# A scan whose later groups keep one PSUM bank instead of reseeding it, with a new instruction order and a one-engine last token

## The chip, the cores and the metric

The kernel runs on one core of a Trainium2 chip (trn2). The metric is the device time of one execution in microseconds (us), the median over several executions. A core has five engines that run their own instruction streams side by side: TensorE (PE, matmuls, with weight loads shown apart as PEld), VectorE (DVE), ScalarE (ACT), GpSimd (POOL) and SyncE (SP, which here only starts transfers). Matmul results go to PSUM, which this kernel treats as eight banks of 512 float32 per partition; ACT and DVE copy them from there to SBUF.

## The reference

Two independent computations over the same length of 2048 tokens and width of 448; their outputs stand side by side in one (1, 2048, 896) bf16 tensor. Part A is a diagonal state-space layer with complex state of 448 entries, part B a local attention with 16 heads of 28, a window of 8 and a dilation of 2.

```python
# A
Lam_bar = jnp.exp(dt * Lam)
B_bar = ((Lam_bar - 1.0) / Lam)[:, None] * Bmat
Bu = jnp.einsum("bld,pd->blp", x + 0j, B_bar)
for t in range(L):
    h = Lam_bar[None, :] * h + Bu[:, t, :]
    hs.append(h)
y = 2.0 * jnp.einsum("blp,dp->bld", hseq, Cmat).real + x * Dskip[None, None, :]
# B
qkv = (x @ wqkv)                       # split into q, k, v and heads
idx = pos[:, None] - off[None, :]      # off = 0, 2, ..., 14; idx < 0 is masked
logits = einsum("bhsd,bhswd->bhsw", q, kg) * scale
attn = softmax(logits)
o = einsum("bhsw,bhswd->bhsd", attn, vg);  b = o @ wo
return concatenate([a, b], axis=-1)
```

## The kernel before

**Units and the order.** The program is put together from 614 *units*. `Planner.add` (L129) makes one: the engine that does it (or a tuple of engines that could), costs, a function that issues its instructions, the units that it depends on, and the PSUM banks or buffers that it takes (`acq`) and gives back (`rel`). The costs and priorities are not used when the program is built: `Planner.run` (L163) walks through a list of unit numbers written out by hand, `ORDER` (L46), and issues each unit in that order. So every engine gets its instructions in the sequence in which its units stand there, and each engine works in that sequence: an instruction that waits holds up everything behind it on its engine. An entry of `ORDER` is the unit's number plus 1000 times the position of the chosen engine in its tuple. A second list, `BANKS` (L77), names the PSUM bank (or the first of a pair) for each `Slot` in the order in which they are first taken.

```python
        for x in ORDER:
            u = self.units[x % 1000]
            ...
            u.on = u.eng[x // 1000]
```

**Part B.** Tokens are handled in two halves, b = 0 and 1, with 128 partitions times 8 tokens each. `loads` (L323) brings weights and x in, the x transposed by DMA (L353). `u_wm` (L434) copies the last 64 columns of the q and k weights into a tile of their own, `wm`, for the mixed projection (`first`, L486). `proj` (L439, matmuls in L453) makes q and k; a tile row has 448 = 3 x 128 + 64 entries, so each output has three full matmuls and 64-row remainders that are done in pairs. Evictions go by `evict` and `copy` (L198 to L210; the copies themselves are L202 on ACT, L206 on DVE, scaled ones L204). `dup` (L532, transfers L535 and L537) copies the k and q of column block 3 within the partition range; it is one unit for each half. `qk` (L539) forms the windowed products on DVE (L560) and sums them on PE (L573), `softmax` (L588) follows; its last step, `turn` (L638), is two copies on ACT for each half that bring the attention weights into the order that `pv` needs. `pv` (L710) multiplies by v on DVE (L727), folds the window (L733 and, for the last group, in halves with L744), turns the result by a DMA transpose (L771), multiplies by wo (full matmuls L790, 64-row remainders L797), and evicts and stores through `ev2` (L800) and `out` (L806). Of the last pair of tokens, the first one's copy goes whole to one engine and the second one's is split, columns 0 to 255 by ACT and the last 192 by DVE (L815 to L819).

**Part A.** `loads` and `load_x` bring the parameters and x (xaT_sb); `setup` forms the discretised factors, `u_s` among them (`spair`, `u6c`), `setup_weights` the input matrix `Bcat`. `powers` (L1068) builds, for each group, diagonal matrices of powers of the factors, `pw`, in two units, the first with 5 powers and the second with 10. Each can go to DVE, as one instruction (L1084), or to ACT, as one for each power and half (L1082).

The scan (L1094) runs over seven groups m of 64 complex states, in 16 phases of tokens, of which each matmul handles 512 columns. The phases are four classes: the even pair P (two banks) and the odd classes 1 and 3 (one bank each). For each group:

1. PE forms the input term in the banks (L1135, 64-row remainders L1138), for the pair first;
2. ACT saves the pair as `eP` (L1148); PE adds it, times a power, to the odd banks (`s1`, L1152);
3. ACT saves bank 1 as `e1` (L1156); PE adds it to bank 3 (L1159); ACT saves part of bank 3 (L1163) and PE adds it (L1167 to L1169);
4. five rounds alternate small copies on ACT (`evv`, L1174) and small products on PE (`l2`, L1179), which carry the state over the row; PE spreads the result (`s4`, L1185) and ACT makes the h of class 3 (`ev3`, L1188);
5. *back to class 1*: PE adds the carried state (`s5`, L1191 and L1192) to bank 1, and ACT copies the h of class 1 out (`ev1f`, through L202);
6. *back to the pair*: the same with `s6` and `s7` (L1231) and a copy of 1024 (`evPf`, L202).

Steps 5 and 6 need the values that steps 2 and 3 had left in bank 1 and in the pair. `FIN` (L43) says for each group and for both where they come from. With `"seed"` the bank is given back as soon as it has been saved, and later ACT copies the saved tile into a fresh bank (`back1`, L1199; `back`, L1217), to which PE then adds. With `"hold"` the bank is kept until the final copy and there is no seed:

```python
            hold, holde = mP == "hold", m1 == "hold"
            s1_, sP_ = (sl[1] if holde else sl["b1"]), (sl["P"] if hold else sl["P2"])
```

Before the change all seven groups use `"seed"` for both. The output product (L1319) then multiplies h with C in units of two tokens; for half of the tokens a skip product with the diagonal is done on PE, for the others on DVE. Copies out of PSUM go through `ev`, stores through `out` (L1341), always begun by SyncE. The last token that the program handles is copied in two pieces, 256 columns by ACT and 192 by DVE (near L1371), and both must be done before its store.

Of the kernel before, what the change touches and what calls it, by code (L numbers as in the profile page):

```python
# [42 lines left out]
FIN = (("seed", "seed"),) * 7  # L43
# [32 lines left out]
]  # L76
BANKS = [  # L77
# [235 lines left out]
class PartB:  # L313
# [114 lines left out]
    def prep(self, u_warm):  # L428
# [5 lines left out]
        self.u_wm = P.add("DVE", vec2(896), lambda: nc.vector.tensor_copy(  # L434
            self.wm[:], self.wqk.rearrange("p k (a c) -> p k a c", a=2)[:, :, :, DF:D]),
# [274 lines left out]
    def pv(self, b, prio, deps):  # L710
# [67 lines left out]
        for j0 in range(0, JB, 2):  # L778
# [27 lines left out]
            def out(j0=j0, jb=jb, e0=0, e1=2):  # L806
                nc.sync.dma_start(self.out_b[b][:, j0 + e0:j0 + e1, :], cx.yb_v[:, jb["y"], e0:e1])
                if e1 == 2:
                    cx.yb_ring.put(jb["y"])
# [3 lines left out]
            en = ("ACT", "DVE")  # L813
            if tail:
                v = P.add(en, (act(448), vec(448)), lambda eng, f=ev2: f(eng, e1=1), [us[2], *cx.u_free], pr, acq="yb")  # L815
                o = P.add("SP", 0.45, lambda f=out: f(e1=1), [v], pr, lat=1.1, dma=0.5)
                w = P.add("ACT", act(D - 192), lambda f=ev2: f("ACT", e0=1, c1=D - 192), [us[2], v], pr)
                w2 = P.add("DVE", vec(192), lambda f=ev2: f("DVE", e0=1, c0=D - 192), [us[2], v], pr)
                P.add("SP", 0.45, lambda f=out: f(e0=1), [w, w2, o], pr, rel=(sl, "yb"), lat=1.1, dma=0.5)  # L819
            else:  # L820
                v = P.add(en, (act(896), vec(896)), ev2, us + cx.u_free, pr, rel=sl, acq="yb")
                P.add("SP", 0.45, out, [v], pr, rel="yb", lat=1.1, dma=1.0)


class PartA:
# [483 lines left out]
    def outputs(self, prio):  # L1309
        nc, pool, P, cx = self.nc, self.pool, self.plan, self.cx  # L1310
        for n, j in enumerate(range(0, T, 2)):
# [29 lines left out]
            def out(j=j, jb=jb, j0=0, j1=2):  # L1341
                nc.sync.dma_start(self.out_a[:, j + j0:j + j1, :], cx.ya_v[:, jb["r"], j0:j1])
                if j1 == 2:
                    cx.ya_ring.put(jb["r"])
# [18 lines left out]
            e = lambda f, **k: (lambda eng: f(eng, **k))  # L1363
            if n < 5:
                v = P.add(*en(896), e(ev), us + x + cx.u_free, pr - 2, rel=sl, acq="ya")
                P.add("SP", 0.45, out, [v], pr, rel="ya", lat=1.1, dma=1.0)
            else:
                u = P.add(*en(448), e(ev, j0=0, j1=1), us[:1] + x + cx.u_free, pr - 2, acq="ya")
                o = P.add("SP", 0.45, lambda f=out: f(j0=0, j1=1), [u], pr, lat=1.1, dma=0.5)
                if n < 7:  # L1370
                    v = [P.add(*en(448), e(ev, j0=1, j1=2), [us[1], u], pr - 2, rel=sl)]  # L1371
                else:
                    v = [P.add("ACT", act(256), lambda f=ev: f("ACT", j0=1, j1=2, c1=256), [us[1], u], pr - 2),
                         P.add("DVE", vec(192), lambda f=ev: f("DVE", j0=1, j1=2, c0=256), [us[1], u], pr - 2)]
                P.add("SP", 0.45, lambda f=out: f(j0=1, j1=2), [*v, o], pr, rel=("ya", sl) if n == 7 else "ya", lat=1.1, dma=0.5)


@with_exitstack
# [103 lines left out]
```

## Time and profile before

| | us |
|---|---|
| runs of the kernel | 135.98, 136.2, 134.9 |
| median | 135.98 |
| the profiled execution's own time | 135.03 |
| its span (first to last instruction or packet of the profile) | 133.3 |
| granted TensorE clock over the span, 1 = full | 0.997 |

The profile is that of one execution, the one of 135.03 us; 1.7 us of it lie outside the span. Times in the profile count from the span's start. A group of instructions is named by the engine, the source line (L1135 is line 1135 of the kernel before), the operation, and the tiles written and read with their shapes. "SPq" and "ACTq" are the sequences in which SyncE and ScalarE start transfers; the length shown there is that of starting one, not of the transfer. In a view by time, each row gives the start, the length to the end of the last instruction, the engine, and the count behind an "x"; a bracket at its end says how long the engine stood idle before it and what ended that. A matmul's end is modelled, so the distance from one start to the next is the surer measure of PE's pace.

### The profile page before, as it was taken

What the parts mean: (1) busy time and instruction counts of PE and PEld (TensorE: products, weight loads), DVE (VectorE), ACT (ScalarE), POOL (GpSimd) and SP (SyncE); (2) the same over time, 40 slices, a digit from 0 to 9 for tenths busy, and PEclk for the clock granted to TensorE, in tenths of its full rate; (3) what the DMA queues carried; (4) which work ended last, traced back from release to release, by engine and by line L of the source; (5) the groups of instructions that cost most, each with busy time, mean ns of one, the idle gap of its engine ahead of it and who ended that gap; (6) DMA issues with size and microseconds to landing.
All of it is one profiled execution on the core that took longest, in us unless ns stands there. A gap on an engine that the chain in (4) does not pass through costs nothing.

```text
span 133.3 us, 2479 instructions
## 1 busy us (share of the span) xinstructions
PE 126.8 (95%) x921; PEld 63.4 (48%) x921; DVE 113.4 (85%) x130; ACT 105.4 (79%) x189; POOL 12.1 (9%) x28
## 2 busy tenths in 40 slices
PE   6999989999999999999999899999999999999990
PEld 2477333434546434464454255444566555545430
DVE  5256998999999999999999999999999999992011
ACT  2067968987999957879999999989999649569270
POOL 6940491000000000000000000000000000000000
PEclk9999999999999999999999999999999999999998
DMA  4999949989346758827869988006620685318642
GB/s 91 207 199 186 146 100 232 178 193 201 73 91 104 170 147 290 222 51 152 266 97 143 260 210 244 19 0 138 147 67 0 165 227 199 102 63 219 234 148 93
DMA packets 47759, 20.25 MB, mean 152 GB/s; under 512 B 38774, under 2 KB 46346, under 8 KB 47748
## 3 DMA queue, kind: packets, MB, share of 16 engines
q1 hardware_dynamic: 46676, 19.77, 64.7%
q10 hardware_dynamic: 880, 0.31, 1.2%
q8 instruction: 7, 0.11, 0.4%
q0 software_dynamic: 192, 0.03, 0.1%
q14 instruction: 4, 0.03, 0.1%
HBM read 5.18 MB, written 4.19 MB: 70 GB/s over the span
## 4 chain that ended last, share of the span: by engine, by line
PE 73%; ACT 15%; SPq 5%; DMA 3%; issue 1%; DVE 0%; ACTq 0%
PE banks L1319 16%; PE banks L1135 12%; PE banks L453 10%; PE banks L790 7%; PE banks L673 7%; PE banks L573 6%; SPq L349 4%; PE banks L1179 3%; DMA rb<-in_B_wqkv_dram 3%; ACT qk L202 2%; ACT pbuf L1174 2%; PE banks L1152 2%; ACT h L202 2%; PE banks L797 2%; ACT banks L1217 1%; SPq L360 1%
## 5 line engine op out<-in xcount | busy, mean ns | idle before, releaser
L560 DVE TENSOR_TENSOR prods<-qk 128x4096 bf16<-128x4096 bf16 (+1 forms) x18 | 31.7, 1809 | 0.3 <-ACT qk L202 0.2
L1135 PE MATMUL banks<-xaT_sb,Bcat 128*128 128x512 bf16 (+1 forms) x112 | 26.9, 381 | 0.6 <-ACT h L202 0.6
L202 ACT CAST ra<-banks 128x896 bf16<-128x896 f32 (+2 forms) x24 | 17.9, 773 | 7.8 <-PE banks L797 4.2
L202 ACT CAST qk<-banks 128x512 bf16<-128x512 f32 (+3 forms) x20 | 16.9, 843 | 3.9 <-PE banks L453 1.4
L733 DVE TENSOR_TENSOR prods<-prods 128x7168 bf16<-128x7168 bf16 x4 | 15.6, 3892 | 0.1
L727 DVE TENSOR_TENSOR prods<-ra 128x7168 bf16<-128x7168 bf16 x4 | 15.5, 3886 | 0.0
L727 DVE TENSOR_TENSOR prods<-ra,qk 128x7168 bf16<-128x7168 bf16 x4 | 15.5, 3886 | 0.1
L1319 PE MATMUL banks<-Ccat,h 128*128 128x448 bf16 x64 | 14.7, 353 | 0.0
L453 PE MATMUL banks<-rb 128*128 128x512 bf16 (+1 forms) x64 | 13.3, 379 | 0.6 <-ACT sh L960 0.6
L1135 PEld LDWEIGHTS <-Bcat 128*128 128x128 bf16 (+1 forms) x112 | 9.1, 100 | 9.7 <-issue 3.7
L673 PE MATMUL banks<-wv,rb 128*128 128x448 bf16 (+1 forms) x64 | 13.7, 354 | 0.0
L1319 PE MATMUL banks<-Ccat,qk 128*128 128x448 bf16 x48 | 11.7, 352 | 0.0
L790 PE MATMUL banks<-wo_p,rb 128*128 128x448 bf16 x48 | 10.9, 354 | 0.0
L1174 ACT CAST pbuf<-banks 128x64 bf16<-128x64 f32 (+1 forms) x42 | 9.3, 229 | 0.9 <-PE banks L1179 0.6
L1179 PE MATMUL banks<-pbuf,pw 128*128 128x64 bf16 x77 | 9.7, 235 | 0.2
L204 ACT ACTIVATE qk<-banks 128x512 bf16<-128x512 f32 (+2 forms) x10 | 8.4, 849 | 1.2 <-PE banks L453 1.0
L1179 PEld LDWEIGHTS <-pw 128*128 128x128 bf16 x77 | 6.5, 105 | 5.5 <-issue 1.9
L453 PEld LDWEIGHTS <-rb 128*128 128x128 bf16 (+1 forms) x64 | 5.1, 96 | 7.9 <-issue 2.8
L206 DVE CAST ra<-banks 128x192 bf16<-128x192 f32 x2 | 0.7, 358 | 9.2 <-ACT ra L202 9.2
L1319 PEld LDWEIGHTS <-h 128*128 128x128 bf16 x64 | 5.8, 98 | 5.3 <-issue 0.7
L1084 DVE TENSOR_TENSOR pw<-Dm,spair 128x1280 bf16<-128x1280 bf16 (+1 forms) x13 | 8.0, 664 | 0.0
L1148 ACT CAST eP<-banks 128x1024 bf16<-128x1024 f32 x7 | 7.1, 1014 | 0.9 <-PE banks L1135 0.9
(145 smaller groups left out, 201.8 us busy)
## 6 DMA issues: line engine op xcount, KB each, us to landing
out_dram<-ra SPq DMA_DIRECT2D x12, 224.0 KB, 2.3
xaT_sb<-in_A_x_dram SPq DMA_DIRECT2D x2, 448.0 KB, 4.8
out_dram<-ra SPq DMA_DIRECT2D x8, 112.0 KB, 1.7
ra<-ra SPq DMA_DIRECT2D x2, 392.0 KB, 4.1
qk<-qk SPq DMA_DIRECT2D x2, 392.0 KB, 4.1
wv<-in_B_wqkv_dram SPq DMA_DIRECT2D x2, 336.0 KB, 4.2
ra<-ra SPq DMA_DIRECT2D x1, 588.0 KB
qk<-qk SPq DMA_DIRECT2D x1, 588.0 KB, 5.6
```

Source lines behind the costliest of these rows:

```text
L202: nc.scalar.copy(out, in_)
L204: nc.scalar.mul(out, in_, scale)
L453: nc.tensor.matmul(out(e)[:, j0:j1], lhsT=w, rhs=self.xB[rows, b, j0:j1, c, :], start=e not in begun, stop=True, skip_group_check=True)
L560: V.tensor_tensor(p[:, :, a:a + n], q[:, t0 + a:t0 + a + n].unsqueeze(1).to_broadcast([NCH, 4, n]), bass.AP(k.tensor, k.offset, [k.ap[0], ...
L673: nc.tensor.matmul(box["ps"][:, e, 0:D], lhsT=self.xB[rows, b, jj, c, :], rhs=self.wv[rows, c, :], start=e not in begun, stop=True, skip_g ...
L727: V.tensor_tensor(out.rearrange("p (u i d h) -> p u i d h", u=4, i=4, d=DH), self.attn[b][:, r].rearrange("p (x u i) h -> p x u i h", x=2, ...
L733: V.tensor_tensor(T1, T1, T2, op=ALU.add)
L790: nc.tensor.matmul(ps, lhsT=o[:, kt + x, :], rhs=self.wo_p[:, (KT + 1) * x + kt, :], start=(kt == 0), stop=False, skip_group_check=True)
L1135: mt(ps(i), lhsT=lhsT, rhs=rhs, start=i not in begun, stop=True, **kw)
L1174: nc.scalar.copy(pb[:, dst, PAD:PAD + NCH // d], tot(a, d))
L1179: mt(tot(out, 2), lhsT=L(T * unit * k), rhs=pb[:, src, PAD - sh:PAD - sh + NCH // 2], start=False, stop=True, **kw)
L1319: nc.tensor.matmul(ps, lhsT=self.h[m][:, i, g * NCH:(g + 1) * NCH], rhs=self.Ccat[:, m, :], start=False, stop=(m == NM - 1), skip_group_ch ...
```

## The change

The diff does these things:

- `FIN`: groups 3, 4, 5 and 6 use `"hold"` for class 1; groups 0 to 2 and all pairs keep `"seed"`. So four units `back1`, one ACT copy each, no longer exist, and bank 1 of those groups stays taken from their input matmuls to `ev1f`.
- `u_wm`, which was DVE's, may be done by ACT too, and in the new order is (entry 1038).
- Stores of both parts may be begun by SyncE or by ACT. In the new order only the very last one (entry 1607, the last token of part A) is begun by ACT.
- The last token of part A is copied by one engine, ACT, in one piece of 448 columns. The last one of part B is copied by one engine too, and with the one before it goes to DVE (entries 1541 and 1543). That is one unit less in each part: 608 instead of 614 in all. The stores of the last tokens no longer wait for the store before them.
- `ORDER` and `BANKS` are new as a whole. Apart from the above, these units change their engine: `dup` for the first half is started by ACT's queue (1084; it was SyncE's), one of the second half's two `turn` units goes from ACT to DVE (1205), and the first `powers` unit of group 3 goes from ACT to DVE (378; it was 1378). The other `turn` unit of the second half stands some twenty ACT units later. The input matmuls and the chain of the scan's first groups stand earlier against part B's work on PE.

```diff
-FIN = (("seed", "seed"),) * 7
+FIN = (('seed', 'seed'), ('seed', 'seed'), ('seed', 'seed'), ('seed', 'hold'), ('seed', 'hold'), ('seed', 'hold'), ('seed', 'hold'))
 ORDER = [
-    22, 2, 5, 0, 1, 6, 23, 7, 1017, 4, 8, 3, 9, 39, 15, 41, 16, 40, 18, 44, 46, 43, 42, 45, 24, 25, 27, 28, 10,
...
+    23, 4, 3, 0, 2, 6, 5, 7, 15, 1017, 1, 45, 16, 18, 43, 46, 42, 44, 39, 40, 41, 24, 59, 57, 47, 61, 60, 58, 8,
...
 BANKS = [
-    0, 0, 2, 3, 5, 0, 2, 4, 0, 6, 4, 2, 6, 0, 4, 6, 2, 4, 2, 6, 4, 6, 0, 4, 7, 6, 2, 4, 7, 5, 4, 2, 5, 6, 2, 5,
...
+    0, 0, 2, 3, 5, 0, 2, 4, 6, 0, 2, 4, 6, 0, 6, 2, 0, 2, 6, 0, 2, 6, 0, 4, 5, 7, 2, 4, 0, 2, 7, 4, 0, 2, 0, 3,
...
-        self.u_wm = P.add("DVE", vec2(896), lambda: nc.vector.tensor_copy(
-            self.wm[:], self.wqk.rearrange("p k (a c) -> p k a c", a=2)[:, :, :, DF:D]),
+        self.u_wm = P.add(("DVE", "ACT"), (vec2(896), act(896) + 0.05), lambda eng: cx.copy(
+            eng, self.wm[:], self.wqk.rearrange("p k (a c) -> p k a c", a=2)[:, :, :, DF:D]),
...
-            def out(j0=j0, jb=jb, e0=0, e1=2):
-                nc.sync.dma_start(self.out_b[b][:, j0 + e0:j0 + e1, :], cx.yb_v[:, jb["y"], e0:e1])
+            def out(eng, j0=j0, jb=jb, e0=0, e1=2):
+                (nc.sync if eng == "SP" else nc.scalar).dma_start(self.out_b[b][:, j0 + e0:j0 + e1, :], cx.yb_v[:, jb["y"], e0:e1])
...
-                w = P.add("ACT", act(D - 192), lambda f=ev2: f("ACT", e0=1, c1=D - 192), [us[2], v], pr)
-                w2 = P.add("DVE", vec(192), lambda f=ev2: f("DVE", e0=1, c0=D - 192), [us[2], v], pr)
-                P.add("SP", 0.45, lambda f=out: f(e0=1), [w, w2, o], pr, rel=(sl, "yb"), lat=1.1, dma=0.5)
+                w = P.add(en, (act(448), vec(448)), lambda eng, f=ev2: f(eng, e0=1), [us[2], v], pr, rel=sl)
+                P.add(*st, lambda eng, f=out: f(eng, e0=1), [w], pr, rel="yb", lat=1.1, dma=0.5)
...
-            def out(j=j, jb=jb, j0=0, j1=2):
-                nc.sync.dma_start(self.out_a[:, j + j0:j + j1, :], cx.ya_v[:, jb["r"], j0:j1])
+            def out(eng, j=j, jb=jb, j0=0, j1=2):
+                (nc.sync if eng == "SP" else nc.scalar).dma_start(self.out_a[:, j + j0:j + j1, :], cx.ya_v[:, jb["r"], j0:j1])
...
-                if n < 7:
-                    v = [P.add(*en(448), e(ev, j0=1, j1=2), [us[1], u], pr - 2, rel=sl)]
-                else:
-                    v = [P.add("ACT", act(256), lambda f=ev: f("ACT", j0=1, j1=2, c1=256), [us[1], u], pr - 2),
-                         P.add("DVE", vec(192), lambda f=ev: f("DVE", j0=1, j1=2, c0=256), [us[1], u], pr - 2)]
-                P.add("SP", 0.45, lambda f=out: f(j0=1, j1=2), [*v, o], pr, rel=("ya", sl) if n == 7 else "ya", lat=1.1, dma=0.5)
+                v = [P.add(*en(448), e(ev, j0=1, j1=2), [us[1], u], pr - 2, rel=sl)]
+                P.add(*st, lambda eng, f=out: f(eng, j0=1, j1=2), v, pr, rel="ya", lat=1.1, dma=0.5)
```

More of the change, by code (lines that the diff above doesn't have):

```diff
@@ L812, in pv @@
             us += [P.add("PE", pe(1, 448), rr, us[:], pr, mode="r")]
-            en = ("ACT", "DVE")
+            en, st = ("ACT", "DVE"), (("SP", "ACT"), (0.45, 0.45))
             if tail:
                 v = P.add(en, (act(448), vec(448)), lambda eng, f=ev2: f(eng, e1=1), [us[2], *cx.u_free], pr, acq="yb")
-                o = P.add("SP", 0.45, lambda f=out: f(e1=1), [v], pr, lat=1.1, dma=0.5)
-                w = P.add("ACT", act(D - 192), lambda f=ev2: f("ACT", e0=1, c1=D - 192), [us[2], v], pr)
-                w2 = P.add("DVE", vec(192), lambda f=ev2: f("DVE", e0=1, c0=D - 192), [us[2], v], pr)
-                P.add("SP", 0.45, lambda f=out: f(e0=1), [w, w2, o], pr, rel=(sl, "yb"), lat=1.1, dma=0.5)
+                P.add(*st, lambda eng, f=out: f(eng, e1=1), [v], pr, lat=1.1, dma=0.5)
+                w = P.add(en, (act(448), vec(448)), lambda eng, f=ev2: f(eng, e0=1), [us[2], v], pr, rel=sl)
+                P.add(*st, lambda eng, f=out: f(eng, e0=1), [w], pr, rel="yb", lat=1.1, dma=0.5)
             else:
                 v = P.add(en, (act(896), vec(896)), ev2, us + cx.u_free, pr, rel=sl, acq="yb")
-                P.add("SP", 0.45, out, [v], pr, rel="yb", lat=1.1, dma=1.0)
+                P.add(*st, out, [v], pr, rel="yb", lat=1.1, dma=1.0)
 class PartA:
@@ L1363, in outputs @@
             e = lambda f, **k: (lambda eng: f(eng, **k))
+            st = ("SP", "ACT"), (0.45, 0.45)
             if n < 5:
                 v = P.add(*en(896), e(ev), us + x + cx.u_free, pr - 2, rel=sl, acq="ya")
-                P.add("SP", 0.45, out, [v], pr, rel="ya", lat=1.1, dma=1.0)
+                P.add(*st, out, [v], pr, rel="ya", lat=1.1, dma=1.0)
             else:
                 u = P.add(*en(448), e(ev, j0=0, j1=1), us[:1] + x + cx.u_free, pr - 2, acq="ya")
-                o = P.add("SP", 0.45, lambda f=out: f(j0=0, j1=1), [u], pr, lat=1.1, dma=0.5)
-                if n < 7:
-                    v = [P.add(*en(448), e(ev, j0=1, j1=2), [us[1], u], pr - 2, rel=sl)]
-                else:
-                    v = [P.add("ACT", act(256), lambda f=ev: f("ACT", j0=1, j1=2, c1=256), [us[1], u], pr - 2),
-                         P.add("DVE", vec(192), lambda f=ev: f("DVE", j0=1, j1=2, c0=256), [us[1], u], pr - 2)]
-                P.add("SP", 0.45, lambda f=out: f(j0=1, j1=2), [*v, o], pr, rel=("ya", sl) if n == 7 else "ya", lat=1.1, dma=0.5)
+                P.add(*st, lambda eng, f=out: f(eng, j0=0, j1=1), [u], pr, lat=1.1, dma=0.5)
+                v = [P.add(*en(448), e(ev, j0=1, j1=2), [us[1], u], pr - 2, rel=sl)]
+                P.add(*st, lambda eng, f=out: f(eng, j0=1, j1=2), v, pr, rel="ya", lat=1.1, dma=0.5)
 @with_exitstack
```

59 rows, old and new, of tables (BANKS, ORDER) are left out of this document.

## The prediction

> **What bounds the kernel now.** I read the page's first part, then the busy times by stage, then TensorE's instructions in order of time, comparing the step from one start to the next with the normal step of the same shape, and last what ScalarE (ACT), VectorE (DVE) and SyncE's queue do at the places found.
>
> ```profile
> span 133.3 us, 2479 instructions
> PE 126.8 (95%) x921; PEld 63.4 (48%) x921; DVE 113.4 (85%) x130; ACT 105.4 (79%) x189; POOL 12.1 (9%) x28
> ...
> 60.00:75.00 15.00, 14.30 (x96) 6.87 (x95) 14.90 (x7) 14.81 (x31) 0.00 (x0) 1.00 0.82 176
> 90.00:105.00 15.00, 14.87 (x120) 8.65 (x119) 14.79 (x6) 14.03 (x32) 0.00 (x0) 1.00 0.33 81
> ```
>
> After the stage's length the columns are PE, PEld, DVE, ACT, POOL, then the granted clock (1.00), DMA share and GB/s. In the scan (60 to 105 us) PE, DVE and ACT are all nearly full; outside it ACT has room. PE sets the end, but only its lost steps can be won:
>
> ```profile
> 8.64 5.25 SPq L353 DMA_TRANSPOSE rb<-in_B_x_dram  x4
> rb<-in_B_x_dram SPq DMA_TRANSPOSE x8, 4.4
> 13.23 3.29 PE L453 MATMUL banks<-rb 128*128 128x512 bf16 x16
> 17.17 3.30 PE L453 MATMUL banks<-rb 64*128 64x512 bf16 x16 [0.65 <-ACT sh L960]
> ...
> 59.43 0.17 PE banks L1185 x3
> 63.39 0.43 PE banks L1152 x2
> 76.50 0.16 PE banks L1192
> ...
> 71.10 0.23 PE L1191 MATMUL banks<-pbuf,pw 128*128 128x128 bf16 x1
> 71.43 0.32 PE L1192 MATMUL banks<-h,pw 128*128 128x384 bf16 x1
> 73.22 0.62 PE L1152 MATMUL banks<-eP,pw 128*128 128x512 bf16 x2
> 73.86 0.33 PE L1185 MATMUL banks<-pbuf,pw 128*128 128x128 bf16 x3
> 74.77 0.81 PE L1135 MATMUL banks<-xaT_sb,Bcat 128*128 128x512 bf16 x3 [0.58 <-ACT h L202]
> 79.40 0.62 PE L1152 MATMUL banks<-eP,pw 128*128 128x512 bf16 x2
> 80.04 0.33 PE L1179 MATMUL banks<-pbuf,pw 128*128 128x64 bf16 x3
> 94.04 0.33 PE L1192 MATMUL banks<-qk,pw 128*128 128x384 bf16 x1
> 94.50 0.33 PE L1179 MATMUL banks<-pbuf,pw 128*128 128x64 bf16 x3
> ```
>
> The three rows of the chain of waits give normal steps: 0.17 for three 128-column matmuls (0.057 each), 0.43 for two of 512 (0.216 each), 0.16 for one of 384. Against them the scan loses 0.74 at 73.86 (0.91 to the next start), 0.27 at 71.10 (0.33), 0.21 at 73.22 and at 79.40 (0.64 each), 0.30 at 94.04 (0.46): 1.73 us, each time a matmul that waits for an ACT copy. At the start, the 16 matmuls from 13.23 are twelve full ones (2.6) and two 64-row pairs (0.44) and a change of tiling (0.10): done by 16.37, so 0.80 is lost before 17.17. The row names ACT L960, which produces nothing for L453; the fourth L353 load, issued near 12.6 and landing 4.4 later, fits.
>
> **The change part by part.**
>
> ```profile
> 113.42 1.70 PE banks L790 x9
> 124.06 2.43 PE L790 MATMUL banks<-wo_p,rb 128*128 128x448 bf16 x12
> 126.43 0.55 PE L797 MATMUL banks<-wo_p,rb 64*128 64x448 bf16 x4
> ...
> 73.70 1.03 ACT L202 CAST h<-banks 128x1024 bf16<-128x1024 f32 x1
> ...
> L1199 ACT CAST banks<-e 128x512 f32<-128x512 bf16 x7 | 4.2, 601 | 0.0
> L202 ACT COPY ra<-ra 128x512 bf16<-128x512 bf16 x4 | 2.4, 621 | 0.0
> L1082 ACT ACTIVATE pw<-Dm,sfac 128x64 bf16<-128x64 bf16 x10 | 2.5, 332 | 0.0
> L202 ACT CAST ra<-banks 128x448 bf16<-128x448 f32 x6 | 3.2, 535 | 2.7 <-PE banks L797 2.0 <-PE banks L1319 0.8
> ...
> L1084 DVE TENSOR_TENSOR pw<-Dm,spair 128x640 bf16<-128x640 bf16 x6 | 2.7, 485 | 0.0
> L434 DVE COPY wm<-rb 128x896 bf16<-128x896 bf16 x1 | 0.4, 384 | 0.0
> ```
>
> *PE's own work.* No matmul is added or removed. But the new order alternates more often between full tiles and tiles of 64 rows or 32 columns: counting neighbours in the two lists, 55 changes become 60. One change: twelve L790 matmuls at 0.189 (nine take 1.70) are 2.27, while L797 starts 2.37 after them: 0.10. Five cost **+0.5**.
>
> *The start.* Before the first unit that needs the L353 loads, PE now does the third 64-row pair too (that of the mixed projection), 0.21 that stood behind the wait. **-0.2**. Its weights come from the L434 copy, now on ACT behind the two evictions that end at about 13.8; the nearest row for its size, the ACT copy of 512 (0.62), and the 1.03 of a 1024 cast bound it, so it is there by 14.8 and PE wants it at 15.2. If that cover failed by x, PE would stand x there. The Sin chain behind it on ACT slips by as much, and DVE has 3 us of products ahead of what needs it.
>
> *The duplicate of k3 and q3 for the first half* goes from SyncE's queue to ACT's:
>
> ```profile
> 25.17 0.53 SPq L535 DMA_DIRECT2D qk<-qk  x1
> 0.80 0.99 ACTq L360 DMA_DIRECT2D rb<-in_B_wqkv_dram  x2
> ```
>
> Two issues, 1.0 us of ACT near 23 us; behind them wait the cast of spair and two projection evictions, whose banks PE asks for some 1.5 us after they would end. No cost. SyncE's queue is 1.1 us earlier with the x loads of part A, which the scan's first group, put some 2.5 us earlier, needs. DVE's kt3 product has four 2 us products ahead of it while the copy lands.
>
> *ACT in the scan.* Four odd seeds (L1199) go: 4 x 0.60, or 0.5 each back to back. One half of the second turn (0.62) goes to DVE, the other behind some twenty copies. The ten L1082 products (2.5 us near 43) go to DVE as one L1084 (0.49); PE lost nothing there, but now group 0's scan units stand up to 3.7 us earlier in PE's order, and that time pays for them. How much of the 1.73 returns? At 74.77 PE waited for the 1.03 us copy at 73.70. That copy has a turn, a seed and a slice copy less ahead of it (0.59 + 0.52 + 0.16 in steps, 1.3 us). PE arrives earlier by 0.74 + 0.27 + 0.21 + 0.2 (start) and by 0.17, since the L1185 unit now stands behind it: 1.6. So about 0.3 stays; the slice copy pushed behind that copy holds the next small product 0.2, and the odd copy of group 2 the s7 product 0.2. Later 2.1 us of seeds and turn are gone and I find no further wait. Of 1.73, 0.7 stays: **-1.0**. Ends: 0 stays (-1.7), or all of it (0).
>
> *The bank that is held.* Without the seed the odd bank stays taken from the input matmuls to the copy of the odd h, and the even pair of the next group must find others. By the new bank list, group 4's pair needs the copy of group 1, group 5's that of group 2, group 6's that of group 3: three of them, as now. I cost it at nothing while ACT ends them in time; else see the rivals.
>
> *DVE* gets L1084 (0.49) and a turn half (nearest row L434, 0.38), loses L434 (0.38), and of the last skip products one more stands ahead of each half of the last fold (0.54 by steps). Its last fold comes about 0.9 later:
>
> ```profile
> 119.45 2.61 SPq L771 DMA_TRANSPOSE rb<-rb  x2
> rb<-rb SPq DMA_TRANSPOSE x2, 2.7
> 119.51 0.62 DVE L744 TENSOR_TENSOR rb<-prods 128x896 bf16<-128x896 bf16 x1
> ```
>
> Its two halves were issued at 119.45 and 120.8 and landed 2.7 later: 122.2 and 123.5, so 123.1 and 124.4 now. Their users have moved back, to 4.4 and 2.9 us ahead of PE's end (seven L790/L797 units and the last seven L1319, by the steps above). That allows a PE end of 127.5; the forecast is 128.9. Covered by 1.4.
>
> *The end.*
>
> ```profile
> 129.00 0.73 PE L1319 MATMUL banks<-Ccat,qk 128*128 128x448 bf16 x3
> 129.77 0.37 ACT L202 CAST ra<-banks 128x256 bf16<-128x256 f32 x1 [0.79 <-PE banks L1319]
> 130.18 0.36 DVE L206 CAST ra<-banks 128x192 bf16<-128x192 f32 x1 [1.34 <-ACT ra L202]
> 130.56 0.33 SPq L1342 DMA_DIRECT2D out_dram<-ra  x1
> ```
>
> The split of the last token did not run side by side: DVE started after ACT. 0.79 from 129.77 to the store becomes one ACT copy of 448 (0.54): -0.25. The store is issued by ACT; SyncE's took 0.33 here, the two ACTq issues above 0.5 each: up to +0.17; I take +0.05, as its shape is SyncE's. **-0.2**. Part B's last token has both copies on DVE; they end about when PE ends, ahead of the last store. Every other store stays on SyncE's queue in the new list; those moved past each other wait on copies that are done some us before.
>
> [...] No run here shows a store from ACT yet.
>
> *Sum:* +0.5 - 0.2 - 1.0 - 0.2 = **-0.9 to -1.0 us**. The profiled execution took 135.03 us, 1.7 around its span of 133.3; it becomes 134.1. It stands 0.95 under the median of the runs, 135.98; against that: **135.0**.
>
> **The rivals.**
>
> *All lost steps return* (ACT's relief reaches each wait): +0.5 - 0.2 - 1.73 - 0.2 = -1.6: **134.3**, with the smaller waits that I did not list about 134.0. For it: 3.1 us less ACT work against 1.73 lost. Against: PE asks earlier too.
>
> *Nothing returns:* the waits move to other copies of the chain, which is as long as before: +0.5 - 0.2 - 0.2 = +0.1: **136.1**. For it: the 60 to 75 row has ACT at 14.81 of 15.
>
> *Slower: the pair of banks comes late.* PE runs in order, so if ACT's last copy of a group ends after PE asks for that pair, PE stands with nothing else. Today this happens once (0.74). If it happens for groups 4, 5 and 6 alike, with nothing won back, 2 x 0.74 is added to +0.1: **137.6**. It decides from about 0.5 us by which ACT is late at each of the three; for it speaks that three banks are now held through the chain, against it that each later group has another 0.5 us less ACT work ahead.
>
> *DVE sets the end.* If PE had headroom all through, the end would follow the last fold: 124.4 + 2.9 + 0.04 + 0.54 + the 2.8 from the issue at 130.56 to the span's end = 130.7, 2.6 less: **133.4**. Against it: L790's and L1319's steps of 0.189 stand back to back without a gap. [...]
>
> **How the numbers follow.** Forecast 0.38 (itself 134.4 to 135.8), all returns 0.27, DVE 0.04, nothing returns 0.17, late banks 0.14. Faster by over 1% (about what a measurement of this kernel can tell from no change) is under 134.6: 0.27 + 0.04 + 0.07 of the forecast's low end = 0.38. Slower is over 137.3: 0.14. The rest, 0.48, lies within. The range, 133.6 to 136.9, leaves the slow rival and half of the DVE one out.
>
> **What would show it.** L1199 x3 instead of x7; ACT's busy time in 75 to 105 lower by 1.5 to 2; the step at group 4's first L1135 near 73.5 with a wait of 0.3, not 0.74; L453's wait 0.6, not 0.8; PE's last start 0.7 to 0.8 earlier; one ACT copy of 448 and an ACTq store at the end. It is wrong if new waits of PE for ACT or DVE of more than 0.5 us appear anywhere between 20 and 60 us, where I expect none, or if the last L771 lands after PE asks.

## The result, and the profile after

The changed kernel takes 147.7 us (median of four runs, 147.5 to 147.93) against 135.72 for the kernel before: 1.089 times as long, 95% interval 1.083 to 1.095. The forecast was 135.0 within 133.6 to 136.9. The profiled execution took 147.90 us. Each experiment below is compared with the kernel before as it ran beside it (median 135.5 to 136.17 there), and its ratio leaves out executions in a slower state (in d_load's comparison 4 of its 13 and 3 of the 17 of the kernel before).

The first lines of the page of the changed kernel, with the busy share of each fortieth of the span (3.66 us) for TensorE, VectorE and ScalarE, and the granted clock:

```profile
span 146.2 us, 2455 instructions
PE 129.3 (88%) x916; PEld 64.7 (44%) x921; DVE 114.0 (78%) x131; ACT 101.2 (69%) x173; POOL 11.4 (8%) x28
...
PE   6999799500599999999999989999999999999990
...
DVE  5258989600069999999999999999999999996020
ACT  3079964000979996657998999898998776784621
...
PEclk9999999975589999999999999999999999999999
```

From the eighth to the eleventh slice, 25.6 to 40.2 us, three engines stand for most of the time, and the granted clock goes down to 0.50 a little later (slices nine to twelve of its row read 7, 5, 5 and 8 tenths). Outside that hole the rows look like those of before. Lines of the changed file stand one or two lower than before: L534 and L535 are the copy of k3 and q3 (L535 and L536 before, not L537 as written ahead), L866 the x loads of part A (L868), L201 the ScalarE copies (L202); the experiments' kernels have shifts of their own, and the text names the work. The view by time, around the hole:

```profile
25.40 6.52 SPq L866 DMA_TRANSPOSE xaT_sb<-in_A_x_dram  x5
...
31.96 1.23 SPq L861 DMA_TRANSPOSE xa_rest<-in_A_x_dram  x1
33.24 6.50 SPq L866 DMA_TRANSPOSE xaT_sb<-in_A_x_dram  x5
34.73 0.48 ACTq L534 DMA_DIRECT2D qk<-qk  x1
36.12 0.47 ACTq L535 DMA_DIRECT2D qk<-qk  x1
36.63 0.54 ACT L201 CAST spair<-sfac 128x420 bf16<-128x420 f32 x1 [13.03 <-DMA xaT_sb<-in_A_x_dram]
...
38.13 1.44 PE L452 MATMUL banks<-rb,wm 128*128 128x512 bf16 x3 [10.47 <-ACT qk L201]
...
41.37 2.29 DVE L559 TENSOR_TENSOR prods<-qk 128x4096 bf16<-128x4096 bf16 x1 [13.57 <-DMA qk<-qk]
```

ScalarE's queue holds the two starts of the copy. It had finished the work ahead of them at 23.6 (36.63 less 13.03), and starts the first at 34.73, the second at 36.12. Everything behind them on ScalarE waits: the spair cast after 13.03 us, then two evictions of part B's projections, and only when the first of these has freed its banks does TensorE go on, after 10.47 us. VectorE's next product reads what is being copied and waits for 13.57 us. What ScalarE waited for is in the row of SyncE above it, and in the chain of waits:

```profile
33.24 2.80 DMA xaT_sb<-in_A_x_dram
...
36.12 0.47 ACTq L535
```

The second start follows the landing, at 36.04, of an x load that SyncE had started at 33.24. In the same way the first, at 34.73, follows the landing at 34.65 of the load of xa_rest started at 31.96. The later load writes xaT_sb, and the copy touches only k3 and q3: no data ties the two. What does is in the instructions of the built program and in the trace. The transfers that SyncE and ScalarE start use eight semaphores there, here S0 to S7, in turn along one listing of both, and the starts below are listed with a wait for the count that the transfer before on the same semaphore brings. In that listing SyncE's loads of x, which wait for no result of an engine, all come ahead of the copy. The trace has the sixteen signals of xa_rest's landing on S7, the last at 34.65, and the sixteen of the x load's on S0, the last at 36.04; each start of the copy follows 0.08 us behind. From the two programs (16 counts for each transfer):

```
changed kernel
SyncE   load xa_rest            waits S7 >= 48                    then S7 = 64
SyncE   x load of part A        waits S0 >= 64                    then S0 = 80
SyncE   5 more x loads, the copy of xa_rest
ScalarE copy of k3              waits S7 >= 64, eviction of k3
ScalarE copy of q3              waits S0 >= 80, eviction of q3
kernel before
SyncE   4 x loads
SyncE   copy of k3              waits S0 >= 48, eviction of k3
SyncE   copy of q3              waits S1 >= 48, eviction of q3
SyncE   4 loads of wv, 2 x loads, xa_rest, 7 x loads, ...
```

On one queue such waits should cost little (an estimate from this trace, not measured by itself): eight starts of SyncE's, at the 0.49 to 1.30 us each that they took between 20 and 41 us, take 4 to 10 us, and the median times from issue to landing were 1.7 to 6.2. Started by ScalarE, the copy waited for loads that SyncE, with 1.3 us for each start, reached 8.4 and 9.6 us after ScalarE was ready at 23.6 (31.96 and 33.24).

The end of the span, in the view by time, is as the diff says: one ScalarE copy of 448 columns, and a store that ScalarE starts.

```profile
142.05 0.73 PE L1317 MATMUL banks<-Ccat,qk 128*128 128x448 bf16 x3
142.82 0.53 ACT L201 CAST ra<-banks 128x448 bf16<-128x448 f32 x1 [2.06 <-PE banks L1317]
143.38 0.37 ACTq L1340 DMA_DIRECT2D out_dram<-ra  x1
```

From the start of the last three matmuls to the end of the span it is 4.15 us (146.2 less 142.05), against 4.30 before.

### The profile page after: what moved, and what is told of

Same layout as the page of the kernel before. It is cut to its first block, busy times and chain, and to the rows that moved or that the text cites. A ratio compares the mean times of both kernels' runs of the same rounds, so it can differ in the third digit from the quotient of the medians.

```text
span 146.2 us, 2455 instructions
## 1 busy us (share of the span) xinstructions
PE 129.3 (88%) x916; PEld 64.7 (44%) x921; DVE 114.0 (78%) x131; ACT 101.2 (69%) x173; POOL 11.4 (8%) x28
## 4 chain that ended last, share of the span: by engine, by line
PE 67%; SPq 21%; DVE 4%; DMA 2%; issue 2%; ACT 1%; ACTq 0%; DVEq 0%
PE banks L1133 16%; PE banks L1317 15%; SPq L866 9%; PE banks L672 7%; PE banks L789 6%; PE banks L1177 4%; SPq L348 4%; SPq L352 3%; PE banks L452 3%; PE banks L572 3%; DVE prods L559 2%; DMA xaT_sb<-in_A_x_dram 2%; PE banks L1150 2%; PE banks L1190 2%; PE banks L796 2%
## 5 line engine op out<-in xcount | busy, mean ns | idle before, releaser
L201 ACT CAST ra<-banks 128x896 bf16<-128x896 f32 (+1 forms) x22 | 17.4, 807 | 8.2 <-PE banks L1317 6.1
L201 ACT CAST qk<-banks 128x512 bf16<-128x512 f32 (+3 forms) x20 | 16.8, 846 | 3.8 <-PE banks L452 2.1
L452 PE MATMUL banks<-rb 128*128 128x512 bf16 (+1 forms) x64 | 14.8, 392 | 0.9 <-ACT sh L958 0.9
L452 PE MATMUL banks<-rb,wm 128*128 128x512 bf16 (+1 forms) x16 | 5.0, 448 | 10.5 <-ACT qk L201 10.5
L201 ACT CAST spair<-sfac 128x420 bf16<-128x420 f32 x1 | 0.5, 542 | 13.0 <-DMA xaT_sb<-in_A_x_dram 13.0
L1082 DVE TENSOR_TENSOR pw<-Dm,spair 128x640 bf16<-128x640 bf16 (+1 forms) x14 | 8.6, 652 | 0.0
```

The lines of the kernel that those rows point to most:

```text
L201: nc.scalar.copy(out, in_)
L452: nc.tensor.matmul(out(e)[:, j0:j1], lhsT=w, rhs=self.xB[rows, b, j0:j1, c, :], start=e not in begun, stop=True, skip_group_check=True)
```

## The experiments

Theory L says that the wait for another queue's transfer, through a shared semaphore, makes the whole loss. Its first rivals: Q, a transfer from ScalarE's queue cannot proceed beside SyncE's run of transposing loads; O, the new order itself puts the copy too late. Then come the size of the loss and the parts of the change that the stall had hidden.

**The copy back on SyncE's queue, in the new order (a_dupSP).** One entry of `ORDER`:

```diff
-    ... 116, 1084, 36, ...
+    ... 116, 84, 36, ...
```

> The changed kernel with one entry of the order put back: the copy of k3 and q3 for the first half is started by SyncE again, at the same place of the order (after six of the x loads of part A). Theory L (the wait stands on ScalarE because its two starts were tied to transfers that SyncE starts 8 to 15 us later): ScalarE's 13.0 us and TensorE's 10.5 us of standing go, and the rest of the change is left: 134.8 us by the terms of my sum (-0.9 against 135.7), between 134 and 137. Rival O (the new order itself puts the copy behind too much, whoever starts it): TensorE still stands over 5 us before 40 us, and the time stays over 141.

Measured: 135.78 us, 1.0022 of the kernel before (0.9991 to 1.0053). The loss is gone, so rival O falls; but so is the gain that I had forecast for the rest of the change. One new loss shows, in TensorE's row at the scan's first group:

```profile
46.33 1.13 PE L1133 MATMUL banks<-xaT_sb,Bcat 64*128 64x512 bf16 x4 [0.17 <-ACT xaT_sb L201]
```

It waits for a ScalarE copy of xaT_sb, which waits for x loads. Counted from start to start, 0.54 us is lost there; with the copy on another queue it is not.

**The copy on ScalarE, with other semaphores (a_lane).** The instructions of each engine stay in the same sequence. One wait is added, so that the program lists the copy ahead of the later x loads: SyncE's fifth x load of part A (the expectation calls it the seventh) waits for the eviction ahead of the copy.

```diff
...
+                if j == 8:
+                    self.cx.tc.add_manual_dep(i.ins, self.b.pre_dup.name, mybir.DependencyInfo(
+                        mybir.DependencyClass.Sync, mybir.DependencyReason.DATA), reason="listed after")
```

In the program built from it the copy's waits become S5 >= 32 and S0 >= 48, counts of loads that were started before 18 us.

> The changed kernel, the copy of k3 and q3 still started by ScalarE, every engine's instructions in the same sequence. One wait is added: SyncE's seventh x load of part A waits for ScalarE's eviction that stands ahead of the copy, so that the program lists the copy ahead of the later x loads and gives it completion semaphores last used by loads of about 16 us. Theory L: ScalarE starts the copy near 24 us at once, the stall of 10.5 on TensorE is gone, and SyncE's later loads are up to 2.5 us later, which can cost part A's first input matmuls up to 1: 134.5 to 137. Rival Q (a start or transfer from ScalarE's queue cannot proceed beside SyncE's run of transposing loads): ScalarE still waits until SyncE's run ends, at 35 us or later, and the time stays at 146 or more.

Measured: 137.26 us, 1.0133 (1.007 to 1.0197), a little over the 134.5 to 137 expected. ScalarE's queue:

```profile
22.49 0.47 ACTq L536 DMA_DIRECT2D qk<-qk  x1
```

This is the second start of the copy, at 22.49, beside SyncE's transposing loads, from the same queue, whose second start had come at 36.12. Rival Q falls. The added wait holds SyncE's loads back, and the first group's 64-row matmuls pay for it, as that expectation said it could:

```profile
46.79 1.13 PE L1137 MATMUL banks<-xaT_sb,Bcat 64*128 64x512 bf16 x4 [1.31 <-ACT xaT_sb L201]
```

**The copy on GpSimd (a_dupPOOL).** In the program built from it the two starts wait for the two evictions and for none of S0 to S7.

```diff
-                q = nc.sync if eng == "SP" else nc.scalar
+                q = nc.sync if eng == "SP" else nc.gpsimd
```

> The changed kernel with the copy of k3 and q3 for the first half started by GpSimd instead of ScalarE; GpSimd has nothing else to do after 21 us, and its transfers use other completion semaphores, so no wait for a transfer of SyncE stands before it. Theory L: 134 to 136, as with SyncE or up to 0.5 better, with the copy landing before 31 us. Rival Q (a transfer beside SyncE's run of transposing loads lands only after it): the copy lands at 38 us or later, VectorE waits over 8 us for it, over 141.

Measured: 135.46 us, 1.0001 (0.9973 to 1.003). GpSimd starts the copy at 21.50 and 22.54, each time with an eviction as the last thing waited for, and VectorE waits 0.41 for it instead of 13.57:

```profile
21.50 0.63 POOL L534 DMA_DIRECT2D qk<-qk  x1 [1.49 <-ACT qk L201]
22.54 0.52 POOL L535 DMA_DIRECT2D qk<-qk  x1 [0.42 <-ACT qk L203]
```

```profile
27.77 3.43 DVE L559 TENSOR_TENSOR prods<-qk 128x4096 bf16<-128x4096 bf16 x2 [0.41 <-DMA qk<-qk]
```

**The kernel before, with the copy on ScalarE and nothing else (b_dupACT).** One entry, 84 to 1084, in the order of before. The program ties the copy to S7 >= 64 and S0 >= 80 here too.

> The kernel before with one entry of the order changed: the copy of k3 and q3 for the first half goes to ScalarE's queue; nothing else. Its listing then ties the two starts to SyncE's tenth and eleventh x loads of part A, which SyncE starts near 31.5 and 32.8 us. Theory L: ScalarE stands from about 25 to about 35.5 us, TensorE 8 to 10 us of it, and a lower granted clock follows: 144 to 147.5 us; this one edit makes the whole loss. My prediction's step (two issues, 1.0 us of ScalarE, no cost): 135.2 to 136.

Measured: 145.68 us, 1.0757 (1.071 to 1.0804). In the list of waits (what waits, for what, us in total, times, longest):

```profile
DVE prods L560 <- PE banks L453: 11.1, 1, 11.1
...
ACT qk L202 <- DMA xaT_sb<-in_A_x_dram: 8.5, 1, 8.5
PE banks L453 <- ACT qk L202: 8.1, 1, 8.1
```

One entry in the list costs 10.2 us without any other part of the change. My prediction's step for it, no cost, is refuted by itself.

**What the hole costs (a_fill, a_fill2).** Is the price the 10.47 us of TensorE, the lower clock behind it, or VectorE's 13.57? These kernels put matmuls with a zero weight tile into TensorE's hole, 40 in the first and 49 in the second, and leave the waits as they are (the lines that make the tile are left out):

```diff
             def dup(eng, b=b):
+                if not b:
+                    for _ in range(40):
+                        nc.tensor.matmul(self.fill_ps, lhsT=self.fill_w[:], rhs=self.xB[:, 0, 0:4, 0, :], start=False,
+                                         stop=True, skip_group_check=True)
```

> The changed kernel as it is, with 40 matmuls of 512 columns more on TensorE in the stretch in which it stands (a zero weight tile, added to a finished bank that ScalarE has yet to copy), 8.6 us at full clock: TensorE is idle for 2 us instead of 10.5, and ScalarE's wait is untouched. Theory C (the idle stretch brings the granted clock down, 0.65 in it and 0.87 in the 12 us behind it, and that costs 1.5 us on top of the 10.5): 145.7 to 146.4, clock 1.00 from 38 to 50 us. Rival (the clock would have dropped anyway, or costs nothing): 147.3 to 147.9.

Measured: 148.2 us, ratio 1.09 (1.083 to 1.098). No gain, but the clock had not stayed up: it was halved from 40.1 to 43.5, behind 2.1 us without matmuls from 36.4 to 38.5. So a second one followed.

> The changed kernel with 49 matmuls more instead of 40 in the stretch in which TensorE stands, so that under 0.6 us of idle is left in it. With 40 the granted clock still fell, to 0.52 at 40 to 42 us and 0.62 at 42 to 44, behind an idle stretch of 2.1, and the time did not move. Theory P (TensorE sets the end, and the half clock costs it 1.6 us): the clock stays 1.00 and the time is 146.0 to 146.5. Theory V (VectorE's 13.6 us of waiting for the copy, less its slack, sets the end by itself): the clock stays 1.00 and the time is 147.3 to 148, with TensorE waiting more elsewhere behind 42 us.

Measured: 148.42 us, 1.095 (1.088 to 1.102), with the clock at 1.00 all through. The half clock cost nothing here: theory P, by which it matters, falls. TensorE's rows show why:

```profile
27.55 10.74 PE L538 MATMUL banks<-rb,fill_w 128*128 128x512 bf16 x49
...
43.07 0.61 PE L580 MATMUL banks<-prods,Zsel 128*32 128x512 bf16 x8
44.20 0.61 PE L580 MATMUL banks<-prods,Zsel 128*32 128x512 bf16 x8 [0.51 <-DVE prods L567]
```

At full speed TensorE comes earlier to the sums at 44.20 and then waits for VectorE's product. So VectorE's wait sets the price. Matched instruction by instruction with a_dupPOOL's trace, VectorE goes on 13.60 us later in the changed kernel (41.37 against 27.77; 0.4 of it stood ahead of the wait), and TensorE's last three matmuls start 13.40 later (142.05 against 128.65). In a_fill2 VectorE goes on at 41.85, another 0.48 later, and the last three matmuls start 0.48 later too:

```profile
128.65 0.73 PE L1317 MATMUL banks<-Ccat,qk 128*128 128x448 bf16 x3
```

```profile
41.85 3.43 DVE L567 TENSOR_TENSOR prods<-qk 128x4096 bf16<-128x4096 bf16 x2 [13.35 <-DMA qk<-qk]
...
142.53 0.73 PE L1325 MATMUL banks<-Ccat,qk 128*128 128x448 bf16 x3
```

The first row is a_dupPOOL's, the others a_fill2's. The medians of the changed kernel and a_dupPOOL are 12.2 apart (147.7 and 135.46), less than the traces, since a_dupPOOL's profiled execution, 134.6, lies 0.9 below its median.

**The seeds (a_seeds).** On the kernel with GpSimd's copy, the four seeds are put back where ScalarE had them before (`FIN` as before, four units more in `ORDER`, four entries more in `BANKS`, so the banks that groups 3 to 6 use for them come with the seeds).

> The changed kernel with the copy of k3 and q3 started by GpSimd (135.46), and in it the four seeds put back: groups 3 to 6 give class 1's bank back and ACT seeds a fresh one, at the places among ACT's instructions where the kernel before had them. The price of the seeds in the new order: theory S (ACT's 4 x 0.60 us stand partly on the path): 0.3 to 1.0 slower than 135.46, with TensorE's lost steps between 60 and 105 us up by as much. Rival H (the held banks cost what the seeds cost, or neither is on the path): within 0.2, and the lost steps unchanged.

Measured: 136.24 us, 1.0032 of before (0.9999 to 1.0066), against 1.0001 without them: 0.4 us, which these runs cannot tell from zero. The traces can: from TensorE's first start behind the wait at 17 us to its last start it is 111.70 without the seeds and 112.70 with them. By stage, without the seeds and with them (columns: PE, PEld, DVE, ACT, POOL, clock, DMA share, GB/s):

```profile
75.00:90.00 15.00, 15.00 (x100) 7.41 (x99) 14.93 (x12) 13.54 (x30) 0.00 (x0) 1.00 0.92 194
90.00:105.00 15.00, 15.00 (x117) 8.43 (x115) 14.90 (x6) 13.27 (x29) 0.00 (x0) 1.00 0.32 93
```

```profile
75.00:90.00 15.00, 14.93 (x98) 7.18 (x97) 14.93 (x12) 14.02 (x31) 0.00 (x0) 1.00 0.97 192
90.00:105.00 15.00, 14.92 (x116) 8.36 (x115) 14.90 (x6) 13.41 (x31) 0.00 (x0) 1.00 0.35 103
```

ScalarE is busier by 0.6 us from 75 to 105 and the rest falls behind 105. Matched matmul by matmul, the two traces keep their distance from the wait at 17 us to 83 us; then TensorE's steps are longer with the seeds, by 0.3 between 84 and 88, 0.2 near 100 and 0.5 later. Theory S, that the four seeds cost time, holds in this pair of traces: the held bank, which saves them, is worth 1.0 us there.

**The tail and the queue alone, on the kernel before (c_tail), and with one held bank (c_best).** The changed code with the order, the seeds and the banks of before, the one-engine copies (part A's on ScalarE, part B's on VectorE), the last store on ScalarE, the copy on GpSimd; then the same with group 5 on `"hold"`.

> The kernel before, with its order and its seeds, and three parts of the change alone: the last tokens copied by one engine each (part A's by ScalarE, part B's by VectorE), the last store begun by ScalarE, and the copy of k3 and q3 for the first half off SyncE's queue, to GpSimd. My tail term: 0.2 earlier from TensorE's last start to the end of the span (4.30 before, 4.1 here); the copy off SyncE's queue: 0 to 0.3. In all 135.0 to 135.4 against 135.5. Rival (a store from ScalarE's queue lands later, or GpSimd's start costs more): 135.5 to 136.

Measured: 135.83 us, 0.9988 (0.9954 to 1.0022): no difference that can be told, where 0.1 to 0.5 less was expected. From the start of the last three matmuls to the end it is 4.24 (129.56 to 133.8), not 4.1. From TensorE's first start behind the wait at 17 us to its last it is 112.66, as much as in a_seeds' trace (112.70), which has the new order with the same seeds and the same queue for the copy: by these traces the new order without the held bank gains nothing there. The trace of before itself has 112.21, so this length differs by 0.4 between traces of one order.

> As the run with the three parts of the change on the kernel before, and group 5 alone keeps class 1's bank (the other groups' banks leave no room for it in this order). One seed of 0.60 less on ScalarE near 93 us, where TensorE lost 0.30 at 94.04: 0.2 to 0.4 less than that run if that wait was the seed's, the same if it moves to another copy.

Measured: 135.87 us, 1.0005 (0.9966 to 1.0044). The step near 95 us is 0.46 in both traces where 0.16 is normal. A single seed less does nothing; the wait there belongs to other copies.

**Fewer changes of tiling (a_merge).** On the kernel with GpSimd's copy, two 64-row pairs of part B's output product are moved to the next pair of their kind.

> The changed kernel with the copy of k3 and q3 started by GpSimd, and two 64-row matmul pairs of part B's output product moved so that they stand beside the next pair of their kind (seven and three TensorE units later; one eviction by ScalarE moves with it). Four changes of tiling less, at 0.10 each: theory M: 0.4 less than that kernel, 134.9 to 135.3, and TensorE's last start 0.4 earlier when counted from the first start behind the wait at 17 us (111.70 there). Rival: the late evictions hold banks that the next matmuls want, and the gain is under 0.1 or turns into a loss.

Measured: 136.48 us, 1.0036 (0.9997 to 1.0076): a miss. One move gives what a change of tiling costs: matmuls that stand 3.07 us later than in the other trace ahead of it stand 2.86 later behind it, 0.10 for each of the two changes. The other loses 1.14, as the distance grows from 1.93 to 3.07; 0.92 of it is one wait:

```profile
99.89 0.55 PE L769 MATMUL banks<-wo_p,rb 64*128 64x448 bf16 x4
100.29 0.91 ACT L174 CAST ra<-banks 128x896 bf16<-128x896 f32 x1 [1.45 <-PE banks L769]
101.09 0.22 ACT L1145 CAST pbuf<-banks 128x64 bf16<-128x64 f32 x1
...
101.36 0.33 PE L1150 MATMUL banks<-pbuf,pw 128*128 128x64 bf16 x3 [0.92 <-ACT pbuf L1145]
```

L769 are the 64-row pairs, L174 their eviction, L1145 and L1150 a slice copy and the small products of the scan. The eviction of the moved pair comes later on ScalarE, the slice copy stands behind it, and TensorE waits for that. It is the same pattern as the big loss, in small: what counts is what is queued behind the thing that moved.

**Earlier x loads at the start (d_load).** On the same kernel, the harmless one of the two moves, and the second pair of part B's weight loads started by GpSimd.

> The changed kernel with the copy of k3 and q3 started by GpSimd (135.46; 1.0001 of before), one pair of 64-row matmuls at the end moved to the next pair (two changes of tiling less, 0.20 by the steps of the run with two such moves), and the second pair of weight loads of part B started by GpSimd near 7.7 us instead of SyncE, so that SyncE starts the six transposing x loads behind it 1.16 us earlier. Theory I (the wait of TensorE at 16 to 17.5 us is set by when SyncE can start the fourth of these loads): TensorE goes on near 16.5 instead of 17.2 to 18.5, and the time is 134.0 to 134.8, 0.7 to 1.3 below before. Rival B (the loads share the DMA engines, which are full from 5 to 14 us, and land when they landed): 135.0 to 135.6.

Measured: 135.81 us, 0.9985 (0.994 to 1.0029). Neither theory is confirmed. In the profiled execution, one of 138.54 us and so 2.7 above the median, a new wait stands ahead of the one in question:

```profile
16.17 3.80 PE L425 MATMUL banks<-rb 128*128 128x512 bf16 x9 [3.07 <-ACT rb L174]
```

TensorE stood 3.07 us for a ScalarE copy that reads the weights that GpSimd loads now; the copy starts at 14.97, where a_dupPOOL has it at 11.05. Why the median did not fall, this one execution can't tell. No version that I tried beats both kernels beyond what the runs can tell.

## Why the prediction was wrong

**The step that failed** is "*The duplicate of k3 and q3 for the first half* goes from SyncE's queue to ACT's": "Two issues, 1.0 us of ACT near 23 us; behind them wait the cast of spair and two projection evictions, whose banks PE asks for some 1.5 us after they would end. No cost." The prediction named its own sign of being wrong, a new wait of TensorE over 0.5 us between 20 and 60 us, and the wait of 10.47 at 38.13 is one. The list of what is queued behind was right, to the unit. What was missing is that the starts themselves could wait, and for a different queue: ScalarE stood 13.03 us for two loads of SyncE's. I priced an instruction by its length and never asked what it must wait for in its new place. The move alone costs 10.2 us in the old order and 12 in the new one; every other term of the sum is 1.0 or less. None of the four rivals had this mechanism; the slower one, three waits for a pair of banks, did not occur.

**The rest, measured with the copy out of the way** (a_dupPOOL, and a_dupSP where it differs), against -0.9 to -1.0 in the forecast:

- *PE's own work, +0.5*: borne out by its two factors. The traces of before and of a_dupPOOL have 55 and 60 changes of tiling, as counted, and a_merge shows 0.10 for one. The term was not measured by itself.
- *The start, -0.2*: not settled. TensorE went on at 17.2, 17.2, 17.3 and 18.4 us in the four traces with the old start, and at 17.3 to 18.5 in seven of the eight with the new one, 19.3 in the eighth. The means are 17.5 and 18.1. The landing of four loads spreads wider than the term, and it can set much of what separates two executions: a_merge's trace leaves the wait 1.93 us behind a_dupPOOL's, and keeps that distance within 0.01 up to 95 us.
- *ACT in the scan, -1.0*: nearly right. All that steps lost against the normal ones from 60 to 105 us, the small losses included, comes to 3.7 before and 2.9 after: -0.8. The wait of 0.74 for group 4's pair is gone. The one that I had put at 0.2, the slice copy behind the copy of group 1's pair, is the largest that is left, 0.57 by the steps:

```profile
72.26 1.09 ACT L201 CAST h<-banks 128x1024 bf16<-128x1024 f32 x1
...
73.03 0.33 PE L1177 MATMUL banks<-pbuf,pw 128*128 128x64 bf16 x3
73.46 0.21 ACT L1172 CAST pbuf<-banks 128x64 bf16<-128x64 f32 x1
...
73.72 0.22 PE L1177 MATMUL banks<-pbuf,pw 128*128 128x64 bf16 x1 [0.35 <-ACT pbuf L1172]
```

- *ACT's busy time* from 75 to 105 fell by 1.4 (28.2 to 26.8), where 1.5 to 2 was forecast. *The bank that is held*, priced at nothing: right, no input matmul of a later group waits for banks in these traces, and the seeds put back cost 1.0.
- *SyncE's queue*: the gain of 1.1 us that I named there matters. With the copy back on it, the x loads come late for the scan's first group, which the new order puts earlier, and 0.54 is lost.
- *DVE*, its last fold covered by 1.4: covered by 1.9 in a_dupPOOL, where the last transpose of the fold lands at 124.43 and the first matmul that reads it starts at 126.34. In the changed kernel it is 1.9 too (137.82 and 139.75): VectorE's lost time does not come in by the last fold but by the products and the softmax of the first half, where TensorE waits for VectorE at 49.31, 0.19 us.
- *The end, -0.2*: about -0.1 (4.30 to 4.15, and 4.24 in c_tail). The store from ScalarE's queue took 0.37 to start, where SyncE's took 0.33. From its start to the end of the span it is 2.8 us, and 2.7 before. So nothing was gained behind the start in this pair of traces.

Behind the start these terms can be checked together. From TensorE's first start behind the wait at 17 us to the end of the span it is 116.15 us in the trace of before and 115.55 in a_dupPOOL's, 0.6 less. The terms give +0.5, -0.8, -0.1 and -0.2 for the pair of matmuls that now stands ahead of the wait, -0.6 in all. The medians show 0.0, within 0.4 either way. So the start must have given back some of it, as the means above would have it, or one pair of traces is not enough; that is not settled. Even without the failed step the forecast of -0.9 was too hopeful, by parts of the scan term and the tail and, it seems, by the start.

## What to carry to other kernels

Moved to ScalarE's queue, the copy kept its waits for the two evictions, and its waits for other transfers became S7 >= 64 and S0 >= 80, counts of late loads of SyncE's: before such a move, read from the built program which semaphores the start waits for, and which queue's transfer must raise them. ScalarE stood 13.03 us for two starts that took 0.48 and 0.47 us themselves, and with it stood all that came behind them on it, so the price to look for is what stands behind a start, not the start's own half microsecond. GpSimd, which had nothing else to do from 20.0 us on, was the safe place for this copy: 135.46 us against 147.7.

## What the runs showed of the hardware that I had not expected

**In the changed kernel the granted clock followed the work 3.5 us late on its way down and 3.2 us late on its way up.** The view by stage of the changed kernel, whose matmuls stop at 27.7 and go on at 38.13 (the third column from the end is the clock):

```profile
28.00:30.00 2.00, 0.00 (x0) 0.00 (x0) 0.00 (x0) 0.00 (x0) 0.00 (x0) 1.00 0.85 171
...
32.00:34.00 2.00, 0.00 (x0) 0.00 (x0) 0.00 (x0) 0.00 (x0) 0.00 (x0) 0.50 0.35 78
...
38.00:40.00 2.00, 1.87 (x5) 0.69 (x5) 0.00 (x0) 1.98 (x4) 0.00 (x0) 0.50 1.11 140
40.00:42.00 2.00, 2.00 (x7) 0.73 (x6) 0.63 (x1) 1.78 (x2) 0.00 (x0) 0.66 1.27 150
42.00:44.00 2.00, 2.00 (x25) 0.61 (x26) 2.00 (x2) 1.15 (x2) 0.00 (x0) 1.00 0.06 12
```

In the trace the clock falls at 31.13, 3.5 us after the last matmul, and comes back at 41.37, 3.2 us after the first. With 40 matmuls in the hole (a_fill) only the 2.1 us from 36.4 to 38.5 have none, and it falls all the same, at 40.10, when matmuls run again:

```profile
36.00:38.00 2.00, 0.41 (x2) 0.10 (x1) 0.00 (x0) 0.98 (x2) 0.00 (x0) 1.00 0.72 139
38.00:40.00 2.00, 1.36 (x6) 0.58 (x6) 0.00 (x0) 1.98 (x4) 0.00 (x0) 1.00 0.97 131
40.00:42.00 2.00, 2.00 (x7) 0.75 (x5) 0.50 (x1) 1.99 (x2) 0.00 (x0) 0.52 1.09 141
42.00:44.00 2.00, 2.00 (x12) 0.41 (x14) 2.00 (x2) 0.76 (x2) 0.00 (x0) 0.62 0.21 40
```

Yet TensorE idled 2.6 us at 17 us in a_merge and 1.9 in c_best, with the clock at 1.00 before and after. So of these three stretches without matmuls, of 1.9, 2.1 and 2.6 us, the clock fell behind the one of 2.1 alone, and only after 1.4 us of matmuls between 38 and 40 at 1.00. What decides between them is not shown here.

**Two executions can repeat each other closely, but need not.** The traces of a_dupPOOL and a_merge, whose orders are the same up to there, keep their distance within 0.01 us over 78 us, from 17 to 95. So a pair of traces can tell parts of 0.1 us apart, where five rounds of times here tell 0.4. But c_tail and c_best, whose programs differ only well behind that, stand 1.11 apart behind the wait at 17 us and 1.52 at 31 us, by a longer wait for a ScalarE eviction in one of them. So the distance has to be followed along the trace before its end is read.
